# Chunk attention, ELU layer and gated layer in one kernel: operand splits moved within a slot, two PSUM banks used by turns, low parts moved from GpSimd to VectorE

## The chip, the cores and the metric

One core of one Trainium2 chip runs the whole program. The metric is the device time of one execution in microseconds (us), the median of several runs. TensorE is written PE, VectorE DVE, ScalarE ACT, GpSimd POOL; SyncE (SP) issues the DMAs.

## What is computed

Eight batches of eight heads, 576 positions, head size 64. Attention runs only within chunks of 64 positions; its output, seen as 4608 tokens of 512 values, goes through an ELU layer (512 to 2048 to 512) and then through a gated layer (512 to twice 1536 to 512).

```python
scores = scale * np.matmul(q_c, k_c.transpose(0, 1, 2, 4, 3))
scores = scores - np.max(scores, axis=-1, keepdims=True)
attn = np.exp(scores)
attn = attn / (np.sum(attn, axis=-1, keepdims=True) + 1e-09)
x = np.matmul(attn, v_c)            # then as [4608, 512]
h = x @ w_in
g = np.where(h > 0.0, h, np.exp(np.minimum(h, 0.0)) - 1.0)
x = g @ w_out
gate = 1.0 / (1.0 + np.exp(-(x @ w_gate)))
out = (gate * (x @ w_val)) @ w_out2
```

The weights arrive as float64 and are converted on the chip.

## The kernel before

Tokens are cut into 9 blocks of 512. Every large product is made from three fp32r products (`PASSES`): each operand is split into a high part (a cast to fp32r) and a low part (the operand minus the high part). A split is therefore one cast and one subtraction, which `split` gives to two engines (lines 90 and 92 are the casts on ACT and DVE, line 96 the subtraction on the engine named).

Phase A runs 144 slots, 16 per block (`slot`, f is the slot's place in its block). One slot holds, in PE's order: an attention product, `layer_1(s)` (12 matmuls into `h`, line 181), in odd slots the transposes of one pair, and `layer_2(s - 2)` (12 matmuls into `y`, line 411). The ELU of slot s runs on ACT and DVE: `elu_exp`, `elu_rest`, then `elu_sum` and `elu_split` in the slot after. Phase B then runs 108 slots of the gated layer (lines 645 to 685), which the change doesn't touch. The order of all instructions on each engine is that of the program text.

The attention of block 0 is done ahead of the slots (`first_block`). The rest goes in 64 pairs, of two groups of 128 positions and two heads each, one pair in two slots. In an even slot: `scores(P)`, softmax (`softmax_max`, `softmax_exp`, `softmax_sum`); in the odd slot after it `transposes(P)` and `transposes_out(P)`; one even slot later `transposes_split(P)`; in the odd slot after that `values(P)` and `values_out(P)`. Pairs 0 to 9 (`P32`; slots 0 to 19, block 0 and a little more) use float32 products of 256 columns, pairs 10 to 63 fp32r products from operands that `split_qkv` splits an odd slot ahead (tiles `kz` and `qv`). For those `transposes_out` sends the halves of `tt` across partitions by two DMAs.

All attention products share one PSUM tile of two banks (`ps_tile`, tag "a", one buffer): each product waits until the one before it has been read. The float32 ones use only the first bank.

In blocks 0 and 8 the weights are converted in the background: `bg(n)` takes n steps, each a DVE instruction with its ACT companions, from a list (9 steps per slot in block 0). At a block's end (f = 15, and f = 0 of the next) the attention output is split into `xs` (`split_x`, four tiles: two low parts on POOL, two on DVE), and `y_out` copies the finished `y` of the block before out in slots f = 1 and f = 2.

On DVE, an odd slot of the fp32r pairs runs `elu_sum`, `values_out`, then in `split_qkv` the cast of k and two subtractions of q and v; an even one runs the cast of `transposes_split`, `elu_sum`, `softmax_max`, `softmax_sum`. POOL has the low part of `kz` (line 241), of `pt` and of `g` (both line 96).

Of the kernel before, what the change touches and what calls it, by code (L numbers as in the profile page):

```python
# [52 lines left out]
def kernel(  # L53
# [141 lines left out]
    def phase_a():  # L195
        with (
# [11 lines left out]

            def ps_tile(name):
                return ps_a.tile([128, 2, 512], F32, tag="a", name=name)  # L210

# [13 lines left out]
            def place(P):  # L225
                j, i = divmod(P, PB)
                hp, c = divmod(i, 2)
                return xr_tile(j + 1, hp), 256 * c

            def split_qkv(P):  # L230

                r = raws.pop(P)
                k = kz[P] = s_p[0].tile([128, 2, 2, 256], F32R, tag="kz", name="kz")
                t = qv[P] = s_p[0].tile([128, 2, 2, 256], F32R, tag="qv", name="qv", bufs=3)
                h0, h1 = halves
                nc.scalar.copy(out=t[h0, :, 0], in_=r[h0, :, 0:256])
                nc.scalar.copy(out=t[h1, :, 1], in_=r[h1, :, 0:256])
                nc.vector.tensor_copy(out=k[:, :, 0], in_=r[:, :, 256:512])  # L238
                nc.vector.tensor_sub(out=t[h1, :, 0], in0=r[h0, :, 0:256], in1=t[h0, :, 0])
                nc.vector.tensor_sub(out=t[h0, :, 1], in0=r[h1, :, 0:256], in1=t[h1, :, 1])  # L240
                nc.gpsimd.tensor_sub(out=k[:, :, 1], in0=r[:, :, 256:512], in1=k[:, :, 0])  # L241

            def scores(P):
                ps = st[P, "s"] = ps_tile("ps_s")
                if P < P32:
                    r = raws.pop(P)
                    for i in range(2):
                        for a in range(2):
                            nc.tensor.matmul(
                                out=ps[:, 0, (2 * i + a) * CH:(2 * i + a + 1) * CH],  # L250
                                lhsT=r[:, i, a * 128:(a + 1) * 128],
                                rhs=r[:, i, 256 + a * CH:256 + (a + 1) * CH],
                                start=True,
                                stop=True,
                            )
                    if P + 1 < P32:
                        load_raw(P + 1)
                    return
                k = kz.pop(P)
                for i in range(2):  # L260
                    for u in range(2):
                        nc.tensor.matmul(  # L262
                            out=ps[:, i, 256 * u:256 * u + 256].rearrange("p (z x) -> p z x", z=2),
                            lhsT=qv[P][:, i, u, 0:128],
                            rhs=k[:, i, :, u * 128:(u + 1) * 128],
                            start=True,
                            stop=True,
                        )
# [12 lines left out]
            def softmax_max(P):  # L281
                s = st[P, "sc"] = a_p.tile([128, 4, CH], F32, tag="s", name="s")
                m = a_p.tile([128, 4, 1], F32, tag="m", name="m")
                ps = st.pop((P, "s"))
                if P < P32:
                    ps = ps[:, 0, 0:256].rearrange("p (n k) -> p n k", n=4)
# [19 lines left out]
            def transposes(P):  # L306
                ps, p = ps_tile("ps_t"), st.pop((P, "p"))
                st[P, "tp"] = ps[:, 0, 0:256]
                for i in range(2):
                    nc.tensor.transpose(  # L310
                        ps[:, 0, 128 * i:128 * i + 128], p[:, 2 * i:2 * i + 2].rearrange("p n k -> p (n k)"), ident,
                    )
# [14 lines left out]
            def transposes_split(P):  # L327
# [5 lines left out]
                    t[:, :, :, 1].rearrange("p u i q -> p (u i) q"),  # L333
                    nc.vector, nc.gpsimd,
                )

            def values(P):
                ps, t = ps_tile("ps_v"), st.pop((P, "t"))
                st[P, "v"] = ps
                if P < P32:  # L340
                    r = vals.pop(P)
                    for i in range(2):
                        for u in range(2):
                            nc.tensor.matmul(
                                out=ps[:, 0, 128 * i + u * CH:128 * i + (u + 1) * CH],
                                lhsT=r[:, i, u * 128:(u + 1) * 128],
# [4 lines left out]
                    load_values(P + 1)  # L351
                    return
                for i in range(2):
                    for u in range(2):
# [9 lines left out]
            def values_out(P):  # L364
                ps, (x, o) = st.pop((P, "v")), place(P)
                if P < P32:
                    nc.scalar.copy(out=x[:, o:o + 256], in_=ps[:, 0, 0:256])
                    return
# [22 lines left out]
            def elu_split(s):  # L391
                g = g_t[s] = g_p.tile([128, 2, TB], F32R, tag="g", name="g")
                split(e_t.pop(s), g[:, 0], g[:, 1], nc.scalar, nc.gpsimd)

# [36 lines left out]
            def slot(s, steps=0):  # L431
# [12 lines left out]
                if even:  # L444
                    if is_pair(P + 1, P32):
                        load_raw(P + 1)
                    if is_pair(P - 1, P32):
                        transposes_split(P - 1)
                    if is_pair(P):
# [14 lines left out]
                if even and is_pair(P):  # L464
                    softmax_max(P)
                if not even and is_pair(V, P32):
                    values_out(V)
                bg(q[0])
# [12 lines left out]
                if last:  # L481
                    split_x(nxt, 1, nc.vector)
                if not even:
                    if is_pair(T):
                        transposes(T)
                    if is_pair(N, P32):
                        split_qkv(N)
                elu_exp(s)
                if even and is_pair(P):
                    softmax_sum(P)  # L490
                bg(q[2])
                if not even and is_pair(T):
                    transposes_out(T)
                elu_rest(s)
# [8 lines left out]
            def first_block(load_w):  # L503
# [28 lines left out]
                for k in range(len(pairs) + 5):  # L532
# [22 lines left out]
                    if (n := at(k - 4)) is not None:  # L555
                        ps = ps_v[n] = ps_tile("ps_v")[:, 0].rearrange("p (n u q) -> p n u q", n=4, u=2)
                        for i in range(2):
# [234 lines left out]
```

## Time and profile before

| | |
|---|---|
| time, median of 3 runs | 1839.76 us (1838.08 to 1840.18) |
| time of the profiled execution | 1839.62 us |
| its span, first to last instruction | 1837.8 us |
| PE busy | 1798.4 us, 98% of the span |
| DVE / ACT / POOL busy | 1014.6 / 724.9 / 412.8 us |
| mean granted PE clock | 0.995 |

A row of a timeline gives start, duration, engine, line, operation, tile written and tiles read, the count of merged instructions, and in brackets the idle time ahead of it with what ended that. A busy time is the sum of durations, and neighbouring instructions can overlap by a little. Lines 90, 92 and 96 are helpers: there the tile's name tells what is done.

### The profile page before, as it was taken

What the parts mean: (1) busy time and instruction counts of PE and PEld (TensorE: products, weight loads), DVE (VectorE), ACT (ScalarE), POOL (GpSimd) and SP (SyncE); (2) the same over time, 40 slices, a digit from 0 to 9 for tenths busy, and PEclk for the clock granted to TensorE, in tenths of its full rate; (3) what the DMA queues carried; (4) which work ended last, traced back from release to release, by engine and by line L of the source; (5) the groups of instructions that cost most, each with busy time, mean ns of one, the idle gap of its engine ahead of it and who ended that gap; (6) DMA issues with size and microseconds to landing.
All of it is one profiled execution on the core that took longest, in us unless ns stands there. A gap on an engine that the chain in (4) does not pass through costs nothing.

```text
span 1837.8 us, 21982 instructions
## 1 busy us (share of the span) xinstructions
PE 1798.4 (98%) x8176; PEld 1481.8 (81%) x8176; DVE 1014.6 (55%) x1671; ACT 724.9 (39%) x1411; POOL 412.8 (22%) x305
## 2 busy tenths in 40 slices
PE   7899999999999999999999999999999999999999
PEld 5778878788787878788888888888888888888887
DVE  6887887787888788876758622223222223132222
ACT  6666665566656566666754301111010101010100
POOL 2223454444444454543220000000000000000000
PEclk9899999999999999999999999999999999999999
DMA  6552121121212221212443100001010101010000
GB/s 215 179 170 94 48 76 53 54 81 46 78 58 66 58 72 53 75 60 82 157 121 122 61 18 23 24 1 46 1 46 1 46 1 46 0 47 0 24 1 23
DMA packets 49498, 111.52 MB, mean 61 GB/s; under 512 B 5872, under 2 KB 17904, under 8 KB 49392
## 3 DMA queue, kind: packets, MB, share of 16 engines
q1 hardware_dynamic: 49392, 110.12, 19.0%
q8 instruction: 65, 1.06, 0.2%
q14 instruction: 41, 0.34, 0.1%
HBM read 84.15 MB, written 18.87 MB: 56 GB/s over the span
## 4 chain that ended last, share of the span: by engine, by line
PE 83%; DVE 8%; ACT 5%; issue 2%; DMA 1%; SPq 0%; DVEq 0%; ACTq 0%
PE o L668 16%; PE pg L181 16%; PE pv L181 16%; PE h L181 16%; PE y L411 15%; PE ps_s L262 1%; DVE qv L240 1%; DVE kz L238 1%; PE ps_v L355 1%; DVE elu L387 1%; DMA tt<-tt 1%; DVE s L294 1%; ACT xs L90 1%; ACT elu L384 1%; DVE t L146 1%
## 5 line engine op out<-in xcount | busy, mean ns | idle before, releaser
L181 PE MATMUL h<-xs,w 128*128 128x512 f32 x1728 | 426.0, 395 | 1.3 <-DVE xs L96 1.3
L411 PE MATMUL y<-g,w 128*128 128x512 f32 x1728 | 424.0, 394 | 0.6 <-DVE y L428 0.6
L657 DVE TENSOR_TENSOR sg<-pv,sg 128x512 f32<-128x512 f32 x108 | 74.6, 691 | 549.8 <-PE pv L181 543.0
L411 PEld LDWEIGHTS y<-g,w 128*128 128x128 f32 x1728 | 319.7, 188 | 66.0 <-DVE y L428 1.0
L181 PEld LDWEIGHTS h<-xs,w 128*128 128x128 f32 x1728 | 317.8, 189 | 64.2 <-DVE xs L96 3.8
L652 ACT ACTIVATE sg<-pg 128x512 f32<-128x512 f32 x108 | 64.4, 597 | 673.5 <-PE pg L181 673.5
L181 PE MATMUL pg<-xs,w 128*128 128x512 f32 x1296 | 311.3, 389 | 0.0
L181 PE MATMUL pv<-xs,w 128*128 128x512 f32 x1296 | 311.3, 389 | 0.0
L668 PE MATMUL o<-w,g 128*128 128x512 f32 x1296 | 311.1, 389 | 0.0
L181 PEld LDWEIGHTS pv<-xs,w 128*128 128x128 f32 x1296 | 243.2, 188 | 50.5
L181 PEld LDWEIGHTS pg<-xs,w 128*128 128x128 f32 x1296 | 243.2, 188 | 50.5
L668 PEld LDWEIGHTS o<-w,g 128*128 128x128 f32 x1296 | 243.2, 188 | 50.5
L96 POOL TENSOR_TENSOR g<-elu,g 128x512 fp32r<-128x512 f32 x144 | 198.7, 1380 | 362.8 <-ACT g L90 353.9
L96 POOL TENSOR_TENSOR xs<-xr,xs 128x512 fp32r<-128x512 f32 x29 | 40.9, 1409 | 814.3 <-ACT xs L90 814.1
L387 DVE SCALAR_TENSOR_TENSOR elu<-h,elu 128x512 f32<-128x512 f32 x144 | 99.5, 691 | 44.6 <-ACT elu L384 42.9
L90 ACT CAST g<-elu 128x512 fp32r<-128x512 f32 x144 | 89.1, 618 | 51.3 <-DVE elu L387 50.4
L241 POOL TENSOR_TENSOR kz<-raw,kz 128x512 fp32r<-128x512 f32 x54 | 96.5, 1787 | 19.1 <-DVE kz L238 16.6
L381 ACT ACTIVATE elu<-h 128x512 f32<-128x512 f32 x144 | 86.0, 597 | 23.0 <-PE h L181 16.6
L96 POOL TENSOR_TENSOR pt<-tt,pt 128x512 fp32r<-128x512 f32 x54 | 70.0, 1297 | 104.9 <-DVE pt L92 98.6
L384 ACT ACTIVATE elu<-elu 128x512 f32<-128x512 f32 x144 | 91.0, 632 | 3.5
L240 DVE TENSOR_TENSOR qv<-raw,qv 64x512 fp32r<-64x512 f32 x54 | 90.3, 1672 | 1.7
L90 ACT CAST w<-t 128x512 fp32r<-128x512 f32 x68 | 42.2, 621 | 95.0 <-DVE t L146 93.8
(74 smaller groups left out, 1465.9 us busy)
## 6 DMA issues: line engine op xcount, KB each, us to landing
raw<-in_qkv SPq DMA_DIRECT2D x54, 512.0 KB, 3.6
wraw<-in_w_out SPq DMA_DIRECT2D x28, 512.0 KB, 3.6
xr<-ymid SPq DMA_DIRECT2D x36, 256.0 KB, 3.6
wraw<-in_w_in SPq DMA_DIRECT2D x16, 512.0 KB, 3.7
ymid<-y SPq DMA_DIRECT2D x32, 256.0 KB, 2.8
out<-o SPq DMA_DIRECT2D x32, 256.0 KB, 2.0
tt<-tt SPq DMA_DIRECT2D x108, 64.0 KB, 2.0
wraw<-in_w_gate SPq DMA_DIRECT2D x12, 512.0 KB, 3.5
```

The source lines that it names most:

```text
L90: nc.scalar.copy(out=out, in_=raw)
L96: lo_eng.tensor_sub(out=lo, in0=raw, in1=hi)
L181: nc.tensor.matmul(out=ps, lhsT=w[:, zw, kk * 128:(kk + 1) * 128], rhs=xs[key, kk][:, zx], start=(kk == 0 and n == 0), stop=(kk == KC - 1 ...
L240: nc.vector.tensor_sub(out=t[h0, :, 1], in0=r[h1, :, 0:256], in1=t[h1, :, 1])
L241: nc.gpsimd.tensor_sub(out=k[:, :, 1], in0=r[:, :, 256:512], in1=k[:, :, 0])
L381: nc.scalar.activation(out=e_t[s], in_=h_t[s], func=ACTF.Exp)
L384: nc.scalar.activation(out=e_t[s], in_=e_t[s], func=ACTF.Relu, scale=-1.0, bias=1.0)
L387: nc.vector.scalar_tensor_tensor(out=e_t[s], in0=h_t.pop(s), scalar=0.0, in1=e_t[s], op0=ALU.max, op1=ALU.subtract,)
L411: nc.tensor.matmul(out=y_t[j, e], lhsT=w[:, zw, e * 128:(e + 1) * 128], rhs=g[:, zx], start=(f == 0 and n == 0), stop=(f == F1 - 1 and n = ...
L652: nc.scalar.activation(out=sg, in_=pg, func=ACTF.Sigmoid)
L657: nc.vector.tensor_tensor(out=sg, in0=pv, in1=sg, op=ALU.mult)
L668: nc.tensor.matmul(out=o_t[t], lhsT=g[:, zx, t * 128:(t + 1) * 128], rhs=w[:, zw], start=(f == 0 and n == 0), stop=(f == F2 - 1 and n == 2),)
```

## The change

Three things move. `split_qkv` is cut in two: `split_k` (the cast of k on DVE) and the rest now stand at the front of the odd slot, around `values_out`, ahead of the ELU's split; before, they came after it and after the transposes. `transposes_split` goes behind `softmax_max` in its even slot, and `transposes_out` goes ahead of the third group of background steps. The subtractions of `kz`, of `pt` and, from slot 16 on, of `g` go from POOL to DVE. And the shared PSUM tile becomes one tile `banks` for the whole of phase A; the float32 products, the transposes and block 0's values take its two banks by turns, while the fp32r products write both.

```diff
-            def ps_tile(name):
-                return ps_a.tile([128, 2, 512], F32, tag="a", name=name)
+            banks = ps_a.tile([128, 2, 512], F32, name="banks")
+            turns = [0]
+            def bank(n):
+                turns[0] ^= 1
+                return banks[:, turns[0], 0:n]
...
+            def split_k(P):
+                k = kz[P] = s_p[0].tile([128, 2, 2, 256], F32R, tag="kz", name="kz")
+                nc.vector.tensor_copy(out=k[:, :, 0], in_=raws[P][:, :, 256:512])
             def split_qkv(P):
...
-                nc.vector.tensor_copy(out=k[:, :, 0], in_=r[:, :, 256:512])
+                nc.vector.tensor_sub(out=k[:, :, 1], in0=r[:, :, 256:512], in1=k[:, :, 0])
                 nc.vector.tensor_sub(out=t[h1, :, 0], in0=r[h0, :, 0:256], in1=t[h0, :, 0])
                 nc.vector.tensor_sub(out=t[h0, :, 1], in0=r[h1, :, 0:256], in1=t[h1, :, 1])
-                nc.gpsimd.tensor_sub(out=k[:, :, 1], in0=r[:, :, 256:512], in1=k[:, :, 0])
             def scores(P):
-                ps = st[P, "s"] = ps_tile("ps_s")
                 if P < P32:
+                    ps, r = bank(256), raws.pop(P)
...
-                ps, p = ps_tile("ps_t"), st.pop((P, "p"))
+                ps, p = bank(256), st.pop((P, "p"))
...
             def transposes_split(P):
...
-                    nc.vector, nc.gpsimd,
+                    nc.vector, nc.vector,
...
-                split(e_t.pop(s), g[:, 0], g[:, 1], nc.scalar, nc.gpsimd)
+                split(e_t.pop(s), g[:, 0], g[:, 1], nc.scalar, nc.gpsimd if s < F1 else nc.vector)
...
                 if even and is_pair(P):
                     softmax_max(P)
-                if not even and is_pair(V, P32):
-                    values_out(V)
+                if even and is_pair(P - 1, P32):
+                    transposes_split(P - 1)
+                if not even:
+                    if is_pair(N, P32):
+                        split_k(N)
+                    if is_pair(V, P32):
+                        values_out(V)
+                    if is_pair(N, P32):
+                        split_qkv(N)
...
-                if not even:
-                    if is_pair(T):
-                        transposes(T)
-                    if is_pair(N, P32):
-                        split_qkv(N)
+                if not even and is_pair(T):
+                    transposes(T)
                 elu_exp(s)
+                if not even and is_pair(T):
+                    transposes_out(T)
                 if even and is_pair(P):
                     softmax_sum(P)
                 bg(q[2])
-                if not even and is_pair(T):
-                    transposes_out(T)
...
-                        ps = ps_v[n] = ps_tile("ps_v")[:, 0].rearrange("p (n u q) -> p n u q", n=4, u=2)
+                        ps = ps_v[n] = bank(512).rearrange("p (n u q) -> p n u q", n=4, u=2)
```

## Rows read from the trace of the kernel before

**Rows 1.** The page, part 1: busy time, share of the span, instructions of each engine

```profile
PE 1798.4 (98%) x8176; PEld 1481.8 (81%) x8176; DVE 1014.6 (55%) x1671; ACT 724.9 (39%) x1411; POOL 412.8 (22%) x305
```

**Rows 2.** Windows: fp32r slots 20 to 126, and one pair of slots; engines' busy time

```profile
182.39:848.75 666.36, 654.43 (x3073) 534.90 (x3071) 534.41 (x816) 406.72 (x829) 318.88 (x223) 1.00 0.21 62
212.59:224.73 12.14, 12.14 (x61) 10.12 (x59) 9.73 (x16) 7.35 (x15) 5.68 (x4) 1.00 0.18 56
```

**Rows 3.** Timeline over the end of block 1 (columns: see the section on the profile)

```profile
243.06 2.90 PE L181 MATMUL h<-xs,w 128*128 128x512 f32 x12
...
248.99 2.90 PE L181 MATMUL h<-xs,w 128*128 128x512 f32 x12
...
255.84 0.39 PE L262 MATMUL ps_s<-kz,qv 128*128 128x256 f32 x1 [0.97 <-POOL kz L241]
...
257.82 0.62 ACT L90 CAST xs<-xr 128x512 fp32r<-128x512 f32 x1
...
270.60 2.93 PE L181 MATMUL h<-xs,w 128*128 128x512 f32 x12
```

**Rows 4.** Timeline of PE over the end of block 6, the last of six

```profile
748.37 2.90 PE L181 MATMUL h<-xs,w 128*128 128x512 f32 x12
...
775.93 1.32 PE L181 MATMUL h<-xs,w 128*128 128x512 f32 x5
```

**Rows 5.** Timeline of DVE in the middle of block 2

```profile
284.58 0.43 DVE L92 CAST pt<-tt 128x512 fp32r<-128x512 f32 x1 [2.34 <-DMA tt<-tt]
```

**Rows 6.** Timeline of DVE and POOL in an undisturbed pair of slots

```profile
206.91 0.43 DVE L92 CAST pt<-tt 128x512 fp32r<-128x512 f32 x1 [0.79 <-DMA tt<-tt]
...
207.98 0.85 DVE L292 TENSOR_TENSOR s<-ps_s,s 64x256 f32<-64x256 f32 x2
...
208.86 0.42 DVE L293 TENSOR_REDUCE m<-s 128x4 f32<-128x256 f32 x1
...
209.31 1.11 DVE L294 TENSOR_TENSOR s<-s,m 128x256 f32<-128x256 f32 x1
...
214.46 1.37 DVE L238 CAST kz<-raw 128x512 fp32r<-128x512 f32 x1
...
215.86 0.69 DVE L239 TENSOR_TENSOR qv<-raw,qv 64x512 fp32r<-64x512 f32 x1
215.91 1.80 POOL L241 TENSOR_TENSOR kz<-raw,kz 128x512 fp32r<-128x512 f32 x1 [0.36 <-DVE kz L238]
...
216.58 1.68 DVE L240 TENSOR_TENSOR qv<-raw,qv 64x512 fp32r<-64x512 f32 x1
```

**Rows 7.** Timeline of DVE, the same line while POOL is idle at its start

```profile
273.12 0.42 DVE L294 TENSOR_TENSOR s<-s,m 128x256 f32<-128x256 f32 x1
```

**Rows 8.** Groups by line over the span (busy, mean ns, idle before with releaser)

```profile
L387 DVE SCALAR_TENSOR_TENSOR elu<-h,elu 128x512 f32<-128x512 f32 x144 | 99.5, 691 | 44.6 <-ACT elu L384 42.9
...
L96 DVE TENSOR_TENSOR g<-sg,g 128x512 fp32r<-128x512 f32 x108 | 74.9, 694 | 3.7
```

**Rows 9.** Waits of PE up to 182 us: total, times, longest

```profile
PE ps_s L249 <- ACT t L319: 12.0, 7, 3.8
```

**Rows 10.** Timeline of DVE in block 0

```profile
46.01 0.42 DVE L287 TENSOR_REDUCE m<-ps_s 128x4 f32<-128x256 f32 x1 [0.33 <-PE ps_s L249]
...
56.59 0.42 DVE L287 TENSOR_REDUCE m<-ps_s 128x4 f32<-128x256 f32 x1 [0.81 <-PE ps_s L249]
...
71.50 0.42 DVE L287 TENSOR_REDUCE m<-ps_s 128x4 f32<-128x256 f32 x1 [0.67 <-PE ps_s L249]
```

**Rows 11.** Chain of waits from 71.4 to 153.3 us, by line

```profile
by line: DVE t L146 11.1%; issue 10.3%; ACT t L124 8.8%; DVE t L140 8.3%; ACT w L90 7.5%; ACT g L90 7.1%; DVE elu L387 6.8%; ACT elu L384 5.2%; DVE w L153 5.1%; DVE t L134 5.0%; ACT elu L381 3.6%; ACT wraw L128 3.5%; DVE d L301 2.7%; DVE m 
```

**Rows 12.** Timeline at the start of block 1

```profile
157.12 2.98 PE L181 MATMUL h<-xs,w 128*128 128x512 f32 x12
157.13 1.62 DVE L96 TENSOR_TENSOR xs<-xr,xs 128x512 fp32r<-128x512 f32 x1 [1.32 <-ACT xs L90]
```

**Rows 13.** DMA issues (count, KB each, median us to landing)

```profile
raw<-in_qkv SPq DMA_DIRECT2D x54, 512.0 KB, 3.6
```

More of the change, by code (lines that the diff above doesn't have):

```diff
@@ L228, in place @@
                 return xr_tile(j + 1, hp), 256 * c
+            def split_k(P):
+                k = kz[P] = s_p[0].tile([128, 2, 2, 256], F32R, tag="kz", name="kz")
+                nc.vector.tensor_copy(out=k[:, :, 0], in_=raws[P][:, :, 256:512])
             def split_qkv(P):
-                r = raws.pop(P)
-                k = kz[P] = s_p[0].tile([128, 2, 2, 256], F32R, tag="kz", name="kz")
+                r, k = raws.pop(P), kz[P]
                 t = qv[P] = s_p[0].tile([128, 2, 2, 256], F32R, tag="qv", name="qv", bufs=3)
@@ L237, in split_qkv @@
                 nc.scalar.copy(out=t[h1, :, 1], in_=r[h1, :, 0:256])
-                nc.vector.tensor_copy(out=k[:, :, 0], in_=r[:, :, 256:512])
+                nc.vector.tensor_sub(out=k[:, :, 1], in0=r[:, :, 256:512], in1=k[:, :, 0])
                 nc.vector.tensor_sub(out=t[h1, :, 0], in0=r[h0, :, 0:256], in1=t[h0, :, 0])
                 nc.vector.tensor_sub(out=t[h0, :, 1], in0=r[h1, :, 0:256], in1=t[h1, :, 1])
-                nc.gpsimd.tensor_sub(out=k[:, :, 1], in0=r[:, :, 256:512], in1=k[:, :, 0])
             def scores(P):
-                ps = st[P, "s"] = ps_tile("ps_s")
                 if P < P32:
-                    r = raws.pop(P)
+                    ps, r = bank(256), raws.pop(P)
+                    st[P, "s"] = ps
                     for i in range(2):
@@ L249, in scores @@
                             nc.tensor.matmul(
-                                out=ps[:, 0, (2 * i + a) * CH:(2 * i + a + 1) * CH],
+                                out=ps[:, (2 * i + a) * CH:(2 * i + a + 1) * CH],
                                 lhsT=r[:, i, a * 128:(a + 1) * 128],
@@ L258, in scores @@
                     return
-                k = kz.pop(P)
+                ps, k = banks, kz.pop(P)
+                st[P, "s"] = ps
                 for i in range(2):
@@ L285, in softmax_max @@
                 if P < P32:
-                    ps = ps[:, 0, 0:256].rearrange("p (n k) -> p n k", n=4)
+                    ps = ps.rearrange("p (n k) -> p n k", n=4)
                     nc.vector.tensor_reduce(out=m[:, :, 0], in_=ps, op=ALU.max, axis=AX.X)
@@ L306, in transposes @@
             def transposes(P):
-                ps, p = ps_tile("ps_t"), st.pop((P, "p"))
-                st[P, "tp"] = ps[:, 0, 0:256]
+                ps, p = bank(256), st.pop((P, "p"))
+                st[P, "tp"] = ps
                 for i in range(2):
                     nc.tensor.transpose(
-                        ps[:, 0, 128 * i:128 * i + 128], p[:, 2 * i:2 * i + 2].rearrange("p n k -> p (n k)"), ident,
+                        ps[:, 128 * i:128 * i + 128], p[:, 2 * i:2 * i + 2].rearrange("p n k -> p (n k)"), ident,
                     )
@@ L333, in transposes_split @@
                     t[:, :, :, 1].rearrange("p u i q -> p (u i) q"),
-                    nc.vector, nc.gpsimd,
+                    nc.vector, nc.vector,
                 )
             def values(P):
-                ps, t = ps_tile("ps_v"), st.pop((P, "t"))
-                st[P, "v"] = ps
+                t = st.pop((P, "t"))
                 if P < P32:
-                    r = vals.pop(P)
+                    ps, r = bank(256), vals.pop(P)
+                    st[P, "v"] = ps
                     for i in range(2):
@@ L344, in values @@
                             nc.tensor.matmul(
-                                out=ps[:, 0, 128 * i + u * CH:128 * i + (u + 1) * CH],
+                                out=ps[:, 128 * i + u * CH:128 * i + (u + 1) * CH],
                                 lhsT=r[:, i, u * 128:(u + 1) * 128],
@@ L352, in values @@
                     return
+                ps = st[P, "v"] = banks
                 for i in range(2):
@@ L366, in values_out @@
                 if P < P32:
-                    nc.scalar.copy(out=x[:, o:o + 256], in_=ps[:, 0, 0:256])
+                    nc.scalar.copy(out=x[:, o:o + 256], in_=ps)
                     return
@@ L446, in slot @@
                         load_raw(P + 1)
-                    if is_pair(P - 1, P32):
-                        transposes_split(P - 1)
                     if is_pair(P):
```

## The prediction

> **What bounds the kernel now.** I read the page first: PE is busy 98% of the span, so only what it loses can be won [rows 1]. Then the timeline of PE, by the distance between the first `layer_1` matmuls of successive slots. In an undisturbed pair of fp32r slots that distance is 12.14 us and PE is busy for all of it, while DVE is busy 9.73 and POOL 5.68 [rows 2]. Phase B runs without a gap and is not touched. So the losses lie in two places.
>
> First, the fp32r slots. From slot 20 to slot 126 there are 53 pairs in 666.36 us [rows 2]. At 12.14 each, less 0.46 because the last has no scores (an estimate, the width of the four scores matmuls), that would be 643.0: PE loses 23.4. The timeline shows where. At the end of block 1, slots f = 14 to f = 2 take 270.60 - 243.06 = 27.54 for two pairs, 3.26 over 24.28; PE waits there for `kz` from POOL, then `qv` and `xs` from DVE [rows 3]. The sixth such end loses 27.56 - 24.28 = 3.28 [rows 4]. Six of 3.27 are 19.6. The remaining 3.8 lie in five single slots inside blocks, after a late transfer: DVE stands 2.34 at the cast of `pt`, first in its even slot, and all behind it, to the next `kz`, comes late [rows 5].
>
> Second, block 0. Seven scores products wait 12.0 us in all for `transposes_out` [rows 9], because one PSUM tile serves every product. But the chain of waits from 71.4 to 153.3 us has no PE in its leading groups: it runs to and fro between DVE and ACT, on weight conversion and ELU [rows 11]. PE's wait is slack there, not loss. A reader who adds up the 12.0 us counts it wrongly.
>
> **DVE's load in a pair.** Added: two low parts of `g`, one of `kz`, one of `pt`, each a 128x512 subtraction. The same on DVE in phase B takes 0.694 [rows 8]; 4 x 0.69 = 2.77. Removed with POOL's work: the cast of `kz` takes 1.37 where the like cast of `pt` takes 0.43; the second `qv` subtraction 1.68 behind a POOL instruction where the first, of the same shape, took 0.69 before that began; the softmax subtraction 1.11 where it took 0.42 with POOL idle [rows 6, 7]. That is 0.94 + 0.99 + 0.69 = 2.62 back. DVE: 9.73 + 2.77 - 2.62 = 9.9 of 12.14. If nothing came back, 12.50. I take 9.9: 1.68 ends 0.55 after POOL's 1.80 does, which is a wait, not work.
>
> The Trainium skill (SBUF — State Buffer, section "SBUF: two separate sides") says that DVE and GpSimd hold a shared port pair exclusively for a whole instruction, DVE whenever it has two SBUF inputs or a two-port mode. By that rule all 2.62 come back, and the two `xs` low parts left on POOL at each block end still block DVE; the four durations above agree with it.
>
> **Undisturbed pairs: no change.** PE's 12.14 stays. Counted from the slot's first product, `qv` should be ready about 4 us into an odd slot of 6.2, and `pt` about 4 us into an even one of 5.93 [rows 3]: the DVE durations in order, after ACT's copies out of PSUM. So nothing gained, nothing lost. New waits: `split_k` heads DVE's odd slot and waits for `raw`, issued on SP about a slot earlier, landing in 3.6 [rows 13]; 2.3 us of cover. Behind it stand `values_out`, the transposes (which need that bank read) and everything else of DVE's slot; without the cover each late microsecond costs up to one. `transposes_out` ahead of the background steps moves nothing here (there are none in blocks 1 to 7); its two DMAs keep their place on SP, and the `raw` load behind them can now go sooner, since its buffer is read sooner, and share the queue with them. `transposes_split` has about 2 us more to its transfer, so a wait of 2.34 shrinks to a few tenths and DVE's 2.2 us of room take that. Of the 3.8 us I take **3.3** back (bounds 1 to 3.8).
>
> **Block ends.** In f = 15 the splits of k, q and v end before the `xs` work instead of after it, so the scores of f = 0 don't wait. What is late next: in f = 0 DVE's first instruction is the low part of the fourth `xs`, which needs ACT's cast; that ended at 258.44, 2.6 after scores began with a second wait inside [rows 3]; I take 2.3. From there to `values`: `xs` low 0.69, `elu_sum` 0.69, two additions 0.85, maximum 0.42, subtraction 0.42, `pt` 0.43 + 0.69 [rows 6 to 8] make 4.2, so `pt` is ready at 6.5 where PE could use it at 5.93: about 0.5 lost. Then `g` low 0.69, `softmax_sum` about 1.0, `elu_sum` 0.69, cast of k 0.43, `values_out` 0.85: 3.7, while the transposes stand 3.2 behind `values` (0.46 of products and 2.74 of `layer_1`, estimates from PE's pace): 0.5 more. After that DVE gains about 1 us per slot. Loss per block end 1.0 (0.5 to 2.2), now 3.27: **6 x 2.27 = 13.6** back (6 to 17).
>
> **Block 0.** With two banks scores wait for `values_out` of the odd slot's front, long done, no more for `transposes_out`. On the DVE and ACT chain this shortens only where DVE itself waited for late scores: 0.33 + 0.81 + 0.67 = 1.8 [rows 10]. PE can also run ahead, until at slot 16 its twelfth `layer_1` matmul needs the low part of `xs`: that ends at 158.75, and the matmul begins about 2.5 after 157.12, at 159.6 [rows 12]. So PE can be another 0.87 earlier: **2.7** (0 to 5: nothing if something else in the chain takes the place, 5 if moving `transposes_out` ahead of the background steps also shortens it).
>
> Sum: 13.6 + 3.3 + 2.7 = 19.6. The profiled execution took 1839.62, its span 1837.8, and the median of the runs is 1839.76, 0.14 more. 1839.6 - 19.6 = **1820**.
>
> **The rivals.**
> *Half cured.* DVE's idle 2.4 us in a pair are waits for ACT and transfers, and don't all go; block ends then pass the loss on from f = 0 to f = 1 and f = 2. For it: in f = 0 DVE stands still until the cast of `xs`. Only the 1.7 of f = 0 is saved, 6 x 1.66 = 10.0, plus 1.6 of the late transfers and 1.8 of block 0: 1826.
> *The turns don't part.* If the wait goes by the whole tile, scores wait as before and block 0 keeps its time: 1839.6 - 16.9 = 1823. Against it: at 157.12 PE starts `layer_1` though the fourth `xs` is whole only at 158.75 [rows 12], so waits go by parts, though that shows it for SBUF only.
> The Trainium skill (PSUM — Partial Sum Buffer, "Summary: rules for kernel authors") advises to read one bank while matmuls write another and to guard by bank; no run here shows it yet.
> *Slower: DVE becomes the bound of every pair.* Place: the fp32r slots. If the 1.37, 1.68 and 1.11 are DVE's own, it has 12.50 of work in 12.14, even with no idle left: 0.36 x 53 = 19 us more, and the block ends give nothing: 1839.6 + 19 - 2 = 1857. It decides from the point where DVE's pair passes 12.14: with 2.62 back, a low part would have to cost 1.25 instead of 0.69; with nothing back, 0.60. Against it are the unblocked durations of the same lines [rows 6, 7].
>
> **Chances.** Forecast (1814 to 1825) 0.70; half cured 0.13; turns not parted 0.05; losses that just offset the gains 0.03; DVE bound 0.09. A change under 0.2%, 3.7 us, can't be told from none here. So faster 0.88, same 0.03, slower 0.09. The range takes in both faster rivals and the bounds of the block ends: 1812 to 1831.
>
> **What would show it.** Right: an undisturbed pair still 12.14 with DVE near 9.9 busy; the cast of k near 0.43 and the `qv` subtraction near 0.7; slots f = 14 to f = 2 within 25.5 instead of 27.5; no PE wait for POOL; scores in block 0 without waits, but block 0 only some 3 us shorter. Wrong: pairs longer than 12.14, DVE waiting for `raw` at `split_k`, or PE waiting for `pt` in ordinary slots.

## The result, and the profile after

The changed kernel takes 1821.37 us (median of 4 runs, 1820.59 to 1821.89) beside 1839.97 (4 runs, 1838.08 to 1840.64) of the kernel before: ratio 0.990, 95% interval 0.9883 to 0.9917. The forecast was 1820.0 in 1812 to 1831. The profiled execution took 1820.99 us with a span of 1819.2, so 18.6 us of span are gone. Lines of `kernel.py` from 208 on have moved by up to ten; line 96 and line 181 stand where they stood.

The page's part 1 of after, to be read beside [rows 1]:

```profile
PE 1790.6 (98%) x8176; PEld 1481.3 (81%) x8176; DVE 1014.3 (56%) x1907; ACT 730.3 (40%) x1411; POOL 74.0 (4%) x69
```

POOL's work fell from 412.8 to 74.0 us, DVE got 236 instructions more, and DVE's busy time is the same: what it took over, it got back from instructions that had become shorter.

Windows of after (stretch, its length, busy time and instructions of PE, PEld, DVE, ACT, POOL, granted PE clock, DMA share, GB/s), over the same slots as [rows 2]:

```profile
182.64:830.08 647.44, 646.03 (x3072) 534.95 (x3071) 524.84 (x1027) 412.09 (x829) 16.54 (x12) 1.00 0.21 63
212.84:224.98 12.14, 12.14 (x60) 10.12 (x59) 9.57 (x20) 7.45 (x15) 0.00 (x0) 1.00 0.21 55
```

Slots 20 to 126 went from 666.36 to 647.44: 18.92 won. Everything up to slot 20 lost 0.25 (its first `layer_1` matmul at 182.64, before 182.39). 18.92 - 0.25 = 18.67, and the span shows 18.6. So the whole gain lies in the fp32r slots and block 0 gave nothing (the start of the same instructions differs by more than 0.25 between runs). An undisturbed pair still takes 12.14, with PE busy for all of it.

The timeline of DVE in that pair, the lines that answer to [rows 6]:

```profile
212.96 0.42 DVE L239 CAST kz<-raw 128x512 fp32r<-128x512 f32 x1
...
214.71 0.69 DVE L247 TENSOR_TENSOR kz<-raw,kz 128x512 fp32r<-128x512 f32 x1
...
216.15 0.69 DVE L249 TENSOR_TENSOR qv<-raw,qv 64x512 fp32r<-64x512 f32 x1
...
221.37 0.42 DVE L303 TENSOR_TENSOR s<-s,m 128x256 f32<-128x256 f32 x1
```

The cast of k fell from 1.37 to 0.42, the second subtraction of q and v from 1.68 to 0.69, the softmax subtraction from 1.11 to 0.42, and the low part of `kz`, now on DVE, takes 0.69.

The timeline at the end of block 1, where before lost 3.26 us [rows 3]:

```profile
252.27 1.42 POOL L96 TENSOR_TENSOR xs<-xr,xs 128x512 fp32r<-128x512 f32 x1 [90.58 <-PE h L181]
252.56 1.68 DVE L249 TENSOR_TENSOR qv<-raw,qv 64x512 fp32r<-64x512 f32 x1
...
254.97 0.63 PE L271 MATMUL banks<-kz,qv 128*128 128x256 f32 x4
255.44 2.92 PE L181 MATMUL h<-xs,w 128*128 128x512 f32 x12
...
257.05 0.69 DVE L96 TENSOR_TENSOR xs<-xr,xs 128x512 fp32r<-128x512 f32 x1 [1.49 <-ACT xs L90]
...
260.51 0.69 DVE L96 TENSOR_TENSOR pt<-tt,pt 128x512 fp32r<-128x512 f32 x1
...
261.26 0.74 PE L365 MATMUL banks<-pt,qv 128*128 128x256 f32 x4 [0.15 <-DVE pt L96]
...
263.78 0.85 DVE L381 TENSOR_TENSOR xr<-banks,s 64x256 f32<-64x256 f32 x2
...
268.28 2.90 PE L181 MATMUL h<-xs,w 128*128 128x512 f32 x12
```

Scores of f = 0 (254.97) no longer wait. What is late next is `pt`, behind DVE's stand of 1.49 for the cast of the fourth `xs`. From 255.44 to 268.28 are 12.84, 0.70 over the pair's 12.14. Counted by distances between `layer_1` matmuls, the six block ends lose 0.66 to 0.69 each, 4.07 in all (19.65 before). And the line of L249 shows what is left of the old slowness: there, while POOL works on `xs`, the second subtraction again takes 1.68.

The waits of PE in after, up to 182 us and then from 182 to 850 (what is waited for, us in total, times, longest), the first to be read beside [rows 9]:

```profile
PE banks L257 <- ACT t L328: 9.0, 7, 2.9
...
PE banks L319 <- ACT xr L377: 2.0, 3, 0.9
...
PE banks L365 <- DVE pt L96: 1.1, 6, 0.2
PE banks L319 <- ACT qv L246: 0.3, 1, 0.3
```

In the fp32r slots PE waits for POOL no more. In block 0 seven scores products still wait for `transposes_out` (12.0 before), and three transposes wait for `values_out`.

### The profile page after: what moved, and what is told of

Read it like the earlier page. It is cut to its first block, busy times and chain, and to the rows that moved or that the text cites. A ratio compares the mean times of both kernels' runs of the same rounds, so it can differ in the third digit from the quotient of the medians.

```text
span 1819.2 us, 21396 instructions
## 1 busy us (share of the span) xinstructions
PE 1790.6 (98%) x8176; PEld 1481.3 (81%) x8176; DVE 1014.3 (56%) x1907; ACT 730.3 (40%) x1411; POOL 74.0 (4%) x69
## 4 chain that ended last, share of the span: by engine, by line
PE 90%; DVE 4%; ACT 4%; DMA 1%; issue 1%; SPq 0%; DVEq 0%; ACTq 0%
PE y L421 19%; PE h L181 18%; PE o L680 16%; PE pg L181 16%; PE pv L181 16%; PE banks L365 1%; PE banks L271 1%; PE banks L319 1%; DVE t L146 1%; DVE elu L397 1%; ACT t L124 1%; DMA qkv<-in_qkv 1%; ACT w L90 0%; DVE t L140 0%; ACT g L90 0%
## 5 line engine op out<-in xcount | busy, mean ns | idle before, releaser
L288 ACT COPY s<-banks 64x256 f32<-64x256 f32 x216 | 79.2, 367 | 142.6 <-PE banks L271 70.9
L96 DVE TENSOR_TENSOR g<-elu,g 128x512 fp32r<-128x512 f32 x128 | 89.5, 700 | 16.9 <-ACT g L90 15.1
L301 DVE TENSOR_TENSOR s<-banks,s 64x256 f32<-64x256 f32 x108 | 45.5, 422 | 67.3 <-ACT s L288 66.6
L96 DVE TENSOR_TENSOR g<-sg,g 128x512 fp32r<-128x512 f32 x108 | 74.9, 694 | 3.7
```

The lines of the kernel that those rows point to most:

```text
L288: nc.scalar.copy(out=t[p], in_=parts_of(st[P, what], p, a)[0])
```

## The experiments

Times are medians, with the kernel before run on the same chip by turns (its medians there 1839.55 to 1840.3). "Slots" is the distance from the first `layer_1` matmul of slot 20 to that of slot 126.

| kernel | us | ratio, 95% | slots | block ends, six |
|---|---|---|---|---|
| after | 1821.37 | 0.9883 to 0.9917 | 647.44 | 4.07 |
| e2, the new order alone | 1827.83 | 0.9918 to 0.9947 | 654.25 | 6.41 |
| e3, the low parts alone | 1826.03 | 0.9913 to 0.9943 | 652.60 | 6.88 |
| e10, after without the turns | 1820.39 | 0.9884 to 0.9917 | 646.97 | 4.17 |
| e1, after, two PSUM tiles up to slot 15 | 1819.55 | 0.9871 to 0.9904 | 647.87 | 4.09 |
| e4, after, `elu_sum` first in f = 0 | 1817.00 | 0.9860 to 0.9889 | 643.84 | 0.02 |
| e5, e1 and e4 | 1815.78 | 0.9847 to 0.9880 | 644.03 | -0.03 |
| e12, e5, two tiles up to slot 17 | 1813.81 | 0.9841 to 0.9874 | 643.39 | 0.04 |
| e11, e5, low parts of block 0's weights on POOL | 1827.62 | 0.9923 to 0.9953 | 644.45 | 0.03 |
| e8, after, low part of `g` twice | 1832.23 | 0.9940 to 0.9969 | 658.85 | 11.01 |
| e9, after, low part of `g` three times | 1871.95 | 1.0161 to 1.0191 | 697.65 | 25.38 |
| e6, after, no sign of the weights | 1814.04 | 0.9840 to 0.9870 | 647.09 | 4.09 |
| e7, e1, no sign of the weights | 1809.99 | 0.9818 to 0.9847 | 648.39 | 4.16 |

### Which of the moves won what

e2 is after with three low parts back on POOL:

```diff
-                nc.vector.tensor_sub(out=k[:, :, 1], in0=r[:, :, 256:512], in1=k[:, :, 0])
+                nc.gpsimd.tensor_sub(out=k[:, :, 1], in0=r[:, :, 256:512], in1=k[:, :, 0])
...
-                    nc.vector, nc.vector,
+                    nc.vector, nc.gpsimd,
...
-                split(e_t.pop(s), g[:, 0], g[:, 1], nc.scalar, nc.gpsimd if s < F1 else nc.vector)
+                split(e_t.pop(s), g[:, 0], g[:, 1], nc.scalar, nc.gpsimd)
```

> The changed kernel with the low parts of kz, pt and g back on POOL: the new order alone. Order theory (splits at the front keep PE from waiting at the block ends, whoever makes the low parts): most of the gain stays, the four slots at a block end lose 1 to 1.7 us instead of 0.67, the late transfers stay covered: about 1825 us. Port theory (the gain is DVE time won back from waiting for POOL): the second qv subtraction stays at 1.7 us, the four slots still lose over 2.5: about 1836 us.

Measured 1827.83, nearer to the order theory's 1825 than to the port theory's 1836. Block ends lose 1.06 to 1.09 each, and behind each of them the slot f = 3 loses a further 0.82 to 0.98. Waits from 182 to 850 us in e2, of PE and of ACT:

```profile
PE banks L365 <- POOL pt L96: 5.0, 6, 0.8
...
ACT elu L391 <- POOL g L96: 14.7, 6, 2.8
```

At the block ends PE waits for the low part of `pt` from POOL, and in f = 3 ACT stands until POOL has read an `elu` tile for the low part of `g`. In an undisturbed pair of e2, over the same slots as the pair of [rows 2], the window and two lines of DVE are:

```profile
212.81:224.95 12.14, 12.14 (x61) 10.12 (x60) 7.93 (x16) 7.46 (x15) 5.50 (x5) 1.00 0.19 56
...
215.39 0.69 DVE L249 TENSOR_TENSOR qv<-raw,qv 64x512 fp32r<-64x512 f32 x1
...
221.34 0.42 DVE L303 TENSOR_TENSOR s<-s,m 128x256 f32<-128x256 f32 x1
```

POOL still works 5.50 us here, yet DVE is busy 7.93 where it was 9.73 before, and these two subtractions take 0.69 and 0.42. The port theory expected the first to stay at 1.7. So the order alone moves them out of POOL's way in such a pair.

e3 is the opposite: the kernel before, with its order and its PSUM tile, and the same three subtractions on DVE:

```diff
-                nc.gpsimd.tensor_sub(out=k[:, :, 1], in0=r[:, :, 256:512], in1=k[:, :, 0])
+                nc.vector.tensor_sub(out=k[:, :, 1], in0=r[:, :, 256:512], in1=k[:, :, 0])
...
-                    nc.vector, nc.gpsimd,
+                    nc.vector, nc.vector,
...
-                split(e_t.pop(s), g[:, 0], g[:, 1], nc.scalar, nc.gpsimd)
+                split(e_t.pop(s), g[:, 0], g[:, 1], nc.scalar, nc.gpsimd if s < F1 else nc.vector)
```

> The kernel before with the low parts of kz, pt and (from slot 16) g on DVE, its old order and its one PSUM tile kept. Order theory: splits still come after the xs work, and the cast of pt still heads DVE's slot, so late transfers still cost 3 us and the block ends lose about 2: about 1831 us. Port theory: DVE is unblocked, so most of the gain comes without the order: about 1823 us.

Measured 1826.03, between the order theory's 1831 and the port theory's 1823. Its block ends lose 1.12 to 1.19, now in the step from f = 15 to f = 0 alone, and four slots f = 3 lose 2.8 in all. Waits from 182 to 850 us in e3, of PE and of ACT, and the time that the DMAs of `tt` took to land:

```profile
PE ps_s L262 <- DVE kz L241: 5.4, 6, 1.0
...
ACT elu L381 <- DMA ymid<-y: 9.3, 6, 1.9
...
DMA to landing us min/median/max: 1.9/2.0/2.1
```

In those f = 3 slots ACT waits, before its first ELU step, for the store of `y` out of the tile that it needs. No transfer of `tt` came late in this run (2.1 at most, 3.6 in before), so e3 does not show what the old order does with a late one. Its undisturbed pair has DVE busy 9.62 with four subtractions more than before: taking the work off POOL also wins the blocked time back.

In the slots the order alone wins 666.36 - 654.25 = 12.1, the low parts alone 13.8, both 18.9. They don't add, 25.9 against 18.9: both shorten the same run of DVE instructions from f = 15 to the `pt` of f = 0, and the 3.27 of a block end can be won once. Neither is idle: without the low parts `pt` comes late from POOL, without the order `kz` comes last on DVE.

### The two banks

e10 undoes the turns in after, and gives every product the rotating tile of before:

```diff
-            banks = ps_a.tile([128, 2, 512], F32, name="banks")
-            turns = [0]
+            def both():
+                return ps_a.tile([128, 2, 512], F32, tag="a", name="banks")
             def bank(n):
-                turns[0] ^= 1
-                return banks[:, turns[0], 0:n]
+                return both()[:, 0, 0:n]
...
-                ps, k = banks, kz.pop(P)
+                ps, k = both(), kz.pop(P)
...
-                ps = st[P, "v"] = banks
+                ps = st[P, "v"] = both()
```

> The changed kernel with the one rotating PSUM tile of before instead of the tile used by turns. If the turns in one tile don't part anything, the time is that of the changed kernel, 1821 us within 1, with the same wait of scores for transposes_out up to slot 15. Rival (the turns do help somewhere): 1823 us or more.

Measured 1820.39, by its interval no different from after, and its waits of PE up to 182 us show the same three figures:

```profile
PE banks L256 <- ACT t L327: 9.0, 7, 2.9
```

So turns within one tile do nothing. The timeline of after shows why (values, then transposes, then scores of successive turns):

```profile
105.06 1.00 PE L353 MATMUL banks<-t,vals 128*128 128x64 f32 x8
...
109.39 0.36 ACT L377 COPY xr<-banks 128x256 f32<-128x256 f32 x1
109.81 0.44 PE L319 MATMUL banks<-ident,p 128*128 128x128 f32 x2 [0.92 <-ACT xr L377]
...
113.47 0.36 ACT L328 COPY t<-banks 128x256 f32<-128x256 f32 x1
113.89 1.10 PE L257 MATMUL banks<-raw 128*128 128x64 f32 x8 [0.89 <-ACT t L328]
```

The transposes write the bank that the values did not, and start 0.06 after the copy of the values ends at 109.75. The scores write the bank that the transposes did not, and start 0.06 after the copy of the transposes ends at 113.83. PE waits each time for the reader of the other bank: the program's waits go by the whole tile. The Trainium skill (PSUM — Partial Sum Buffer, "Summary: rules for kernel authors") advises to guard by bank; a guard by tile, as here, doesn't give what that rule is for.

e1 gives these products real turns: each takes a one-bank tile of its own from a pool of two, up to slot 15, and the two-bank tile is made at slot 16.

```diff
             def bank(n):
+                if "one" in ps_of:
+                    return ps_of["one"].tile([128, 512], F32, tag="one", name="one")[:, 0:n]
                 turns[0] ^= 1
-                return banks[:, turns[0], 0:n]
+                return ps_of["banks"][:, turns[0], 0:n]
...
+                tc.tile_pool(name="ps_one", bufs=2, space=bass.MemoryType.PSUM) as ps_one,
...
+                del ps_of["one"]
+                ps_of["banks"] = ps_a.tile([128, 2, 512], F32, name="banks")
                 for s in range(F1, (NB - 1) * F1):
```

> The changed kernel, but up to slot 15 the products that used a bank by turns take a PSUM tile of their own each (two buffers of one bank), so that scores really wait only for the product two before. Chain theory (block 0 is bound by the DVE and ACT round trip, PE's wait for transposes_out is slack): the wait of scores for transposes_out up to slot 15 goes from 9.0 us to under 1, but block 0 gets only 1.8 to 2.7 us shorter, about 1819 us. Rival (PE's 9.0 us of waits are lost time): about 1812 us. If the time stays at 1821 with the waits gone, even the 1.8 us on the chain were no loss.

Measured 1819.55, 1.8 below after. The waits for `transposes_out` up to slot 15 are gone. Slot 2 begins at 51.73 instead of 56.30, so the two waits ahead of it, 5.7 of the 9.0, lay for the most part on the path. This start differs from run to run, but the ranges are apart: 50.96 to 53.09 in the five kernels with two tiles, 54.72 to 57.45 in the nine with one. From slot 2 to slot 16 it takes 102.24, and 100.46 without a stand of 1.78 at the end, against 101.07: there the other five waits, 3.3, and the 2.0 of the transposes were slack but for 0.6. PE now waits for something else instead, the low part of `g`, which POOL still makes in block 0:

```profile
PE y L422 <- POOL g L96: 3.3, 5, 1.3
```

The stand of 1.78 is at the change of tiles, where the scores of slot 16 wait for the last reader of the small tiles; slot 16 is 3.4 ahead, slot 20 only 1.8.

The timeline of PE at that place in e1, and two windows, up to the end of the stand and behind it (columns as above):

```profile
153.06 1.10 PE L258 MATMUL banks<-raw 128*128 128x64 f32 x8 [1.78 <-ACT t L329]
153.97 4.58 PE L181 MATMUL h<-xs,w 128*128 128x512 f32 x12
```

```profile
148.00:153.00 5.00, 3.08 (x13) 1.99 (x11) 4.25 (x7) 3.20 (x8) 1.71 (x2) 1.00 0.11 12
155.00:158.00 3.00, 3.00 (x8) 2.30 (x7) 2.53 (x4) 1.03 (x2) 1.04 (x2) 0.50 0.00 0
```

The twelve matmuls take 4.58, in after 2.98, without a wait: the granted clock behind the stand was 0.50, the lower level of 1.2 GHz, where it was 1.00 (2.4 GHz) before. It fell in e5 behind the same stand of 1.78 and in e11 behind one of 3.18 (0.50 each), and not in e7, where the stand at this place is 0.25.

e12 keeps the small tiles two slots longer (with e4's move below), so that the change of tiles has no late reader in front of it:

```diff
-                for s in range(F1, (NB - 1) * F1):
+                for s in range(F1, 2 * P32 - 2):
                     slot(s)
+                del ps_of["one"]
...
+                    ps_of["banks"] = ps_a.tile([128, 2, 512], F32, name="banks")
+                    for s in range(2 * P32 - 2, (NB - 1) * F1):
```

> Two tiles and elu_sum first (1815.8 us), with the two tiles kept up to slot 17, where the fp32r products begin, instead of slot 15. In the run with two tiles PE stood 1.78 us at the change of tiles before slot 16 and then ran its layer_1 group at a granted clock of 0.68 and 0.54: 4.4 us instead of 2.7. If that wait brought the clock down, the scores of slot 16 start without it, the clock stays at 1.00 and another 1 to 1.6 us are won: about 1814.5 us. Rival: PE now stands as long inside slot 16, until the fourth xs is split (that bound stays), the clock falls all the same, and the time is 1815.8 within 0.5.

Measured 1813.81, 2.0 below e5 and the fastest of the kernels that do the whole computation. The timeline of PE at slot 16 of e12, and a window over its `layer_1`:

```profile
151.37 2.86 PE L181 MATMUL h<-xs,w 128*128 128x512 f32 x8
155.09 1.20 PE L181 MATMUL h<-xs,w 128*128 128x512 f32 x4 [0.86 <-POOL xs L96]
156.13 2.90 PE L422 MATMUL y<-g,w 128*128 128x512 f32 x12
```

```profile
151.40:156.10 4.70, 3.63 (x14) 2.08 (x14) 3.74 (x5) 3.08 (x7) 4.70 (x4) 1.00 0.32 112
```

Slot 16 starts 2.6 earlier than in e1; PE stands 0.86 for `xs` (1.07 idle in the window) and stays at full clock. The next `layer_2` begins at 156.13 instead of 158.40.

### Block ends

e4 swaps two steps in f = 0, so that DVE does `elu_sum` while it would stand for the cast of `xs`:

```diff
-                if f == 0 and j > 0:
-                    split_x(j, KC - 1, nc.vector)
                 if s > 0:
                     elu_sum(s - 1)
+                if f == 0 and j > 0:
+                    split_x(j, KC - 1, nc.vector)
```

> The changed kernel with elu_sum ahead of the split of the fourth xs in slot f = 0, so that DVE does it while ACT casts. If PE's last loss at the block ends is the DVE chain from that split to pt (0.69 of it is elu_sum): the wait of 0.15 to 0.20 for pt at f = 1 goes, and slots f = 0 to f = 2 lose under 0.2 instead of 0.67 us: 6 x 0.5 = 3 us, about 1818 us. Rival (the loss hangs on ACT or on values_out, not on this chain): no change, 1821 us.

Measured 1817.00. The timeline of e4 at the end of block 1:

```profile
256.29 0.69 DVE L397 SCALAR_TENSOR_TENSOR elu<-h,elu 128x512 f32<-128x512 f32 x1
...
257.76 0.69 DVE L96 TENSOR_TENSOR xs<-xr,xs 128x512 fp32r<-128x512 f32 x1 [0.77 <-ACT xs L90]
...
261.68 0.63 PE L365 MATMUL banks<-pt,qv 128*128 128x256 f32 x4
```

`elu_sum` (line 397) fills half of the stand, `values` start without a wait, and the six block ends lose 0.02 in all. So the rest of a block end was the order of these two instructions, as the prediction's step said of `pt`. The slots are 3.6 shorter, not 4.0, as three slots f = 3 lose 1.0 in all behind the store of `y`, where one lost 0.46 in after; the medians, 4.4 apart, also hold the differences of the start.

e5 is e1 and e4 together, to see whether the two gains add:

```diff
+                    return ps_of["one"].tile([128, 512], F32, tag="one", name="one")[:, 0:n]
...
+                if f == 0 and j > 0:
+                    split_x(j, KC - 1, nc.vector)
```

> Two tiles up to slot 15 and elu_sum ahead of the split of the fourth xs, together, on top of the changed kernel. If the two gains (1.8 and 4.4 us against 1821.4) lie in different stretches, block 0 and the block ends, they add: 1815.2 us, block ends at 0, the span to the first layer_1 of slot 20 as with two tiles alone. Rival (both only move PE's start against DVE, so they overlap): 1817 us.

Measured 1815.78, 5.6 below after; e1 gave 1.8 and e4 4.4, 6.2 together. They lie in different stretches and very nearly add.

### DVE's room, and POOL in DVE's way

e8 and e9 compute the low part of `g` once and twice more, in blocks 1 to 7 (e8 has `range(1)`, e9 `range(2)`):

```diff
-                split(e_t.pop(s), g[:, 0], g[:, 1], nc.scalar, nc.gpsimd if s < F1 else nc.vector)
+                e = e_t.pop(s)
+                split(e, g[:, 0], g[:, 1], nc.scalar, nc.gpsimd if s < F1 else nc.vector)
+                if F1 <= s < NB * F1 - F1:
+                    for _ in range(1):
+                        nc.vector.tensor_sub(out=g[:, 1], in0=e, in1=g[:, 0])
```

> The changed kernel with the low part of g computed twice on DVE in blocks 1 to 7: 2 x 0.69 us more per pair, 9.6 + 1.4 = 11.0 of 12.14. If DVE bounds a pair only when its busy time passes 12.14, undisturbed pairs stay 12.14 and only the block ends lose more, 1.5 to 2.5 us instead of 0.67, because DVE catches up more slowly: 1826 to 1832 us. Rival (its waits for ACT, some 1.5 us a pair, count as well): every pair longer by 0.2 to 0.5, 1835 to 1850 us.

> The changed kernel with the low part of g computed three times on DVE in blocks 1 to 7: 9.6 + 2.8 = 12.3 us of work in 12.14. This is the point at which DVE should become the bound of every pair. By busy time alone a pair takes 12.3 to 12.4, some 10 us more over 53 pairs, and block ends never recover: 1840 to 1850 us. Rival (neighbouring instructions overlap by about 0.08 us each, so busy time overstates DVE's work by more than 1 us a pair): pairs stay at 12.14 and the time under 1842. Rival (waits for ACT count as well): pairs of 13 us and more, over 1860.

Measured 1832.23 and 1871.95. A window over one undisturbed pair of e8 and the longest of PE's waits from 182 to 850 us in it:

```profile
212.00:224.14 12.14, 12.14 (x60) 10.13 (x59) 10.88 (x22) 7.44 (x15) 0.00 (x0) 1.00 0.19 55
```

```profile
PE h L181 <- DVE xs L96: 5.3, 6, 0.9
```

The same of e9:

```profile
206.71:219.40 12.69, 12.31 (x61) 10.05 (x60) 12.16 (x23) 7.58 (x15) 0.00 (x0) 1.00 0.20 55
```

```profile
PE banks L319 <- DVE xr L381: 23.0, 46, 1.2
PE h L181 <- DVE xs L96: 11.8, 6, 2.0
```

With 1.3 us more of DVE work (9.57 to 10.88) the pair keeps its 12.14; the block ends pay, 11.01 instead of 4.07, and the pairs behind them, 5.1 in all. With 1.3 more (12.16) every pair takes 12.69: DVE sets the pace, at 0.53 over its busy time. This is the slower rival, made by hand. The time, 1871.95, is 22 above the upper end of what was expected for busy time alone. Of the 50.2 us that the slots of e9 take more than those of after, ordinary pairs hold only 18.4; block ends lose 25.38 instead of 4.07, and the six pairs behind them 11.0 instead of 0.5: there is no room left to catch up.

e11 gives POOL the low parts of block 0's 32 weight tiles, with e5 as its base:

```diff
-            nc.vector.tensor_sub(out=w[:, 1], in0=parts.pop(n).bitcast(F32), in1=w[:, 0])
+            low_eng.tensor_sub(out=w[:, 1], in0=parts.pop(n).bitcast(F32), in1=w[:, 0])
...
-                first_block(convert(tiles, conv_p, len(W_AT), 6))
+                first_block(convert(tiles, conv_p, len(W_AT), 6, nc.gpsimd))
```

> Two tiles and elu_sum first (1815.8 us), and in block 0 the low parts of the converted weights on POOL too: 32 subtractions of 0.69 us less on DVE. Chain theory (DVE's work bounds block 0): up to as much as without the sign step, 5 us less, 1811 us. Rival (POOL's 1.3 to 1.8 us each block DVE's own subtractions and hold the weights back): 1816 to 1822 us.

Measured 1827.62, 11.8 slower than e5 and slower than either theory expected. Groups by line and shape (busy, mean ns, idle before) in block 0 of e11, from 60 to 165 us, where 24 of the 32 fall:

```profile
L153 POOL TENSOR_TENSOR w<-t,w 128x512 fp32r<-128x512 f32 x24 | 34.3, 1442 | 4.9 <-ACT w L90 4.9
L140 DVE SCALAR_TENSOR_TENSOR t<-wraw,t 128x512 uint32<-128x512 uint32 x23 | 24.5, 1064 | 0.5
L137 DVE TENSOR_SCALAR t<-t 128x512 uint32<-128x512 uint32 x22 | 13.7, 624 | 0.0
```

and the same of e5, from 60 to 155 us:

```profile
L153 DVE TENSOR_TENSOR w<-t,w 128x512 fp32r<-128x512 f32 x24 | 16.3, 681 | 0.0
L140 DVE SCALAR_TENSOR_TENSOR t<-wraw,t 128x512 uint32<-128x512 uint32 x23 | 15.7, 681 | 0.0
L137 DVE TENSOR_SCALAR t<-t 128x512 uint32<-128x512 uint32 x22 | 9.2, 416 | 0.0
```

DVE's own instructions grow from 681 to 1064 ns and from 416 to 624: of the 16.3 us taken away 8.8 + 4.5 come back in these two lines and 3.8 in a third (line 134, 418 to 590), so DVE has won nothing, and each tile's low part takes POOL's 1442 ns besides. Slots 2 to 16 take 112.55 instead of 102.21, 1.4 of it in a longer stand at the change of tiles (3.18).

e6 and e7 ask whether block 0's waits for PSUM matter once the chain of DVE and ACT is shorter. They leave out the step that puts the sign back on the weights, in after and in e1:

```diff
-            steps = ((sign, n - 1), (clamp, n), (add, n - 1), (shift, n), (rest, n - 2))
+            steps = ((None, n - 1), (clamp, n), (add, n - 1), (shift, n), (rest, n - 2))
...
-                        step is clamp and low(m), step is shift and magnitude(m + 1), step(m),
+                        step is clamp and low(m), step is shift and magnitude(m + 1), step and step(m),
```

> The changed kernel without the step that puts the sign back into the converted weights (32 DVE instructions of about 0.6 us apart in block 0; the weights are then all positive). Chain theory (DVE and ACT bound block 0): each pair of slots in block 0 sheds up to 3.6 x 0.6 = 2.2 us and comes near PE's own 12.7, so the 101.1 us from slot 2 to slot 16 fall to 90 to 94, about 1812 us. Rival (PE's waits on the one tile bound block 0): the 101.1 stay within 2.

> The same without the sign step, but with two tiles up to slot 15. Chain theory: with DVE lighter the single tile starts to matter; against the one-tile run without sign the stretch up to slot 20 is 2 to 5 us shorter. Rival (the tile never matters beyond the 1.8 us of the start): 1.8 us shorter, no more.

Measured 1814.04 and 1809.99. Without the step, slots 2 to 16 take 95.44 instead of 101.07 with one tile (90 to 94 was expected), and 93.35 with two. So the conversion bounds block 0, though not by DVE's busy time alone: 5.6 us were won for a step that takes 15.7 in e5's row of line 140. With the chain shorter two tiles are worth 4.05 instead of 1.8. Not all of this is the chain: e7 has neither e1's stand nor its lower clock at the change of tiles. Up to slot 16 alone two tiles win 2.1 here and, without the stand, 0.6 there.

## Why the prediction was right, and where it was not

The time came out 1.4 us above the forecast, the sum of the terms 1.0 too high (19.6 told, 18.6 measured in the span). Two of its terms were wrong and nearly cancelled: block ends gave 2.0 more than told, block 0 2.7 less and 0.25 lost besides. That the total came out this close is partly luck.

**DVE's load** was right: 12.14 for the pair, DVE at 9.57 where 9.9 was told. The three blocked instructions got back 0.95 + 0.99 + 0.69 = 2.63 of the 2.62 told. That was not the work of the moved subtractions alone: e2 shows the new order winning most of it with POOL still at work (DVE 7.93). The 0.3 by which DVE is lower is the softmax subtraction of the pair in [rows 2], which took 1.39 there and 1.11 in the pair of [rows 6]. The Trainium skill (SBUF — State Buffer, "SBUF: two separate sides") has the rule that one of DVE and GpSimd holds the shared ports for a whole instruction. The traces agree with it: 1.68 is back at block ends where POOL works, and 416 ns become 624 in e11.

**Undisturbed pairs** were right: no change, and in the fp32r slots no instruction waits for `raw` at `split_k`.

**Late transfers** came out as told, 3.3 (the 3.75 outside block ends became 0.41), with one of the five slots misread. Four of them, 3.0 us, stand behind a late `tt`. The fifth, slot 82, lost 0.87 as PE waited for the copy of the last block's `y`. Its line in before, and then, for after, the longest time of a `tt` to land from 182 to 850 us and ACT in slot 67:

```profile
579.83 0.96 PE L411 MATMUL y<-g,w 128*128 128x512 f32 x3 [0.56 <-DVE y L428]
```

```profile
DMA to landing us min/median/max: 1.9/2.0/4.0
...
469.82 0.60 ACT L391 ACTIVATE elu<-h 128x512 f32<-128x512 f32 x1 [2.06 <-DMA ymid<-y]
```

In after a `tt` took up to 4.0 to land (3.6 in before), and DVE waited for one only once, 1.0: the later cast covers them, as the prediction said, and all five slots are clean. Slot 67 loses 0.46 to the store of `y`, which no term held.

**Block ends** had the right mechanism and a size that was too small: 15.6 back, 13.6 told. The step that was mis-sized is the loss after the move, told as 0.5 + 0.5, measured as 0.46 up to the values of f = 1 and 0.23 behind them. The chain to `pt` was right within 0.3: `pt` was to be ready 6.5 after scores began and was ready 6.23 after (261.20 - 254.97), the fourth `xs` starting at 2.08, not 2.3. The second term, the transposes' 0.5, was too high because it adds up durations whose neighbours overlap: the same instructions sum to 3.67 in after, as told, but `values_out` ended 3.43 behind `pt` (263.78 + 0.85 - 261.20).

**Block 0** was wrong: 2.7 told, nothing came. The step that failed is "with two banks scores wait for `values_out` of the odd slot's front, long done, no more for `transposes_out`". They still wait, 9.0 us in seven waits. The rival that the turns don't part, held at 0.05, is what the mechanism did; by its own sum (1823) it is 1.6 above the measured time, since it took the block ends at 13.6. The reason against it was misread from [rows 12]: the four `xs` are four tiles, so that `layer_1` may start before the fourth is whole says nothing of the parts of one tile, and the first matmul that reads the fourth began at 159.26, after its low part ended at 158.75. A block end of before does show a wait by parts in SBUF (there that matmul began at 258.92, ahead of the low part's end at 259.69), but the prediction had no row on a PSUM tile. The other half, that most of PE's 12.0 is slack, was right for the slots behind slot 2 and not for the two waits ahead of them: with real turns e1 was 4.6 earlier at slot 2, 0.6 better up to slot 16 without its stand.

**The rivals.** *Half cured* was not the case: losses pass on from f = 0 only as 0.46 and 0.23. *DVE as the bound* was not the case by 2.6 us per pair, and e8 and e9 put the point between 10.88 and 12.16 of busy DVE work in a pair. The prediction put it at 12.14 with no idle left; as e9 runs at 0.53 more than its busy time, an estimate from its row is 12.14 - 0.53 = 11.6. Its price was reckoned too low: it left the block ends at before's 19.65, where e9 lost 25.38 there and 11.0 in the pairs behind them.

What stays open: with two tiles PE's longest wait in block 0 is for the low part of `g` from POOL (3.3 in e1), and no run moved that one to DVE.

## What to carry to other kernels

Two buffers in one tile are two buffers only if the waits see them as two: where a product still starts right after the reader of the other half, as the scores here did 0.06 us after the copy, give each half its own tile. A subtraction that takes POOL 1.3 us and DVE 0.7 can cost DVE as much when it stays on POOL (9.73 us in a pair of before, 9.62 in e3 with four of them moved), because DVE's own steps grow while POOL runs; compare a line's duration with POOL idle and busy before dividing work, and see whether an order keeps the two apart (7.93 in e2). And where an engine stands while ready work is behind it, put a step that is ready ahead of one that waits for another engine: e4's swap of two steps took the block ends from 4.07 to nothing.

## What the runs showed of the hardware that was not expected

A PE that got ahead was slowed. In e1 it reached slot 16 early, stood 1.78 us in one piece, and the granted clock behind that fell to 0.50. From the first `layer_1` matmul to the first `layer_2` matmul slot 16 then took 158.40 - 153.97 = 4.43, in after, at 1.00, 160.19 - 157.37 = 2.82, so some 1.6 us went to the clock. The same fall came in e5 (1.78) and e11 (3.18); with a stand of 0.86 in e12 and of 0.25 in e7 the clock stayed at 1.00. These are comparisons of kernels, not a run that sets the clock alone.

And POOL held up DVE instructions with one input as well as those with two: the cast of k (1.37 against 0.42) and the `TENSOR_SCALAR` steps of e11 (624 against 416 ns).
